# A fused top-k attention and feed-forward kernel: the feed-forward's steps from queues with conditions to a fixed list over four slots

## The chip, the cores and the metric

The kernel runs on one core of a Trainium2 chip. The metric is the device time of one execution in microseconds (us). Before the change the median of three runs is 1399.42 us (1398.67 to 1402.97).

The engines are named as in the profile: PE is TensorE (PEld its weight loads), DVE is VectorE, ACT is ScalarE, POOL is GpSimd, SP is SyncE, which here only issues DMAs. PE writes its results to PSUM, where the kernel's tiles take one bank (512 float32 columns) or two.

## What is computed

```python
# q, k, v: batch 8, heads 8, sequence 576, head size 64
scores = scale * np.matmul(q, k.transpose(0, 1, 3, 2))
kth = np.partition(scores, -32, axis=-1)[..., -32:-31]
scores = np.where(scores >= kth, scores, -1e9)
attn = np.exp(scores - np.max(scores, axis=-1, keepdims=True))
attn = attn / (np.sum(attn, axis=-1, keepdims=True) + 1e-09)
attn_out = np.matmul(attn, v)
# x: (4608 tokens, 512), the heads of a token side by side
h = x @ w_in            # w_in: 512 x 2048
g = h * np.cos(h)
out = g @ w_out         # w_out: 2048 x 512
```

The two weights come as float64; the kernel loads their words and rebuilds float32 from them ("decoding").

## The kernel before

**Units and slots.** The 4608 tokens are cut into 36 blocks of 128, the heads into 4 pairs. A unit is one block with one pair of heads: 128 rows, two times 576 scores. The 144 units run through a software pipeline with one unit a slot (`slot`, line 755); four slots make one block. The order in the program is the order in which each engine works, since the scheduling is manual. Slots are told apart by their number modulo 4 (0 to 3).

**Attention in a slot.** For the unit of slot i (`u`), DVE searches the 32 largest scores of each row: the row is folded in half into larger and lesser members (`fold_high`, line 261, makes the larger ones in `rest` from PSUM and from a copy `s`; POOL makes the lesser ones in `low` with `fold_sum`, line 279, and `fold_low`, line 287), then `topk_round` takes eight at a time with MAX8 and strikes them out with MATCH_REPLACE8: four searches in `rest`, and last two in `low`. The first slots that also decode weights (`BUSY`, slots 8 to 10) make `low` on DVE instead (`fold_now`, line 271). For the unit before (`w`), DVE merges the lists (`merge_first`, `merge_second`, lines 344 and 351), and ACT masks (`mask`, line 374) and exponentiates (`exponentials`, line 383), which leaves the sums of the rows; DVE ends the slot with the sums (line 395) and the reciprocal `rden` (line 400). For the unit before that (`x`), `send` (line 740) has POOL split the words of the probabilities and of the reciprocal into halves (`split`, line 405, two copies, lines 410 and 412), and SP writes them to memory and reads them back transposed into one of five places of `ring`. In the first six slots the transposes are done on PE instead (`turn`). PE makes the scores of two units in every second slot (slots 0 and 2, `scores`, line 235), and ACT copies those of the next unit out of PSUM (`take_scores`, line 250). In slot 2 PE multiplies the four transposed units of a block with V (P@V, `values`, line 456), and DVE scales the result into `xT` (`take_values`, line 481).

**PSUM.** Scores have two tiles of two banks, the tile `rim` (the last score columns and P@V) has two banks; two more banks, tag `mm`, serve both products of the feed-forward.

**Feed-forward.** The first product of a block (`ff1`, line 537) makes four banks of 128x512, each in two items; the second product (`ff2`, line 619) adds 16 chunks into one bank, in items of two chunks. ACT empties a bank of the first product with two instructions (`take_first`, line 566: `g`, and `x` as an integer, the number of turns). The argument of the cosine is reduced on POOL (`reduce_first`, line 590, makes `x` float, `reduce_second`, line 599, subtracts), ACT takes the sine (`sines`, line 602), POOL multiplies (`gate`, line 612), all on tiles of 128x1024, two for a block. `take_second` (line 638) scales the result and writes it out.

**What sets the order.** Items wait in the queues `first` and `second`; in each slot `feed` takes them by a plan, and `can_first` and `can_second` let an item go only if its inputs were made enough ticks ago:

```python
    plan = (
        ((0, 0), (1,), (1,)),
        ((0, 0), (1, 1), (0,)),
        ((0,), (1,), ()),
        ((1, 0, 0), (1, 1), ()),
    )
```

Here 0 is an item of the first product and 1 one of the second; the three groups of a slot stand ahead of the scores, behind the top-k's last round, and at the slot's end. Full banks are emptied wherever `take_banks` is called. After the last slot, `drain` and `forward` run what is left, with the cosine's argument and the gate on DVE.

**Weights.** `load_weights` (line 103) loads chunks, `decode_first` (ACT, at a slot's end), `decode_second` (DVE, line 151) and `decode_third` (POOL, line 160) rebuild them in this and the next slot.

Of the kernel before, what the change touches and what calls it, by code (L numbers as in the profile page):

```python
# [30 lines left out]
def kernel(  # L31
# [64 lines left out]
    ff = {"live": 0, "tick": 0, "now": 0, "end": False, "kind": 0, "half": 0, "open": 0, "late": False}  # L96
# [213 lines left out]
    def topk_first(u, w):  # L310

        u["top"] = tops[u["n"] % len(tops)]
        if w:
            merge_first(w)
        if u["n"] not in BUSY:
            fold_sum(u)
        fold_high(u)
        if w:
            merge_second(w)
        if u["n"] in BUSY:  # L320
            fold_now(u)
        topk_round(u, 0, [lambda: distances(w), lambda: None] if w else ())
# [82 lines left out]
    def split(u):  # L405


        s = u.pop("s").rearrange("p j k -> p (j k)").bitcast(U16)
        halves = work.tile([P, 2, 2 * S + P], U16, tag="halves", name="halves", bufs=1)
        nc.gpsimd.tensor_copy(out=halves[:, :, 0 : 2 * S], in_=s.rearrange("p (k h) -> p h k", h=2))  # L410
        rden = u.pop("rden").bitcast(U16).rearrange("p (j h) -> p h j", h=2)
        nc.gpsimd.tensor_copy(
            out=halves[:, :, 2 * S :].rearrange("p h (j d) -> p h j d", j=2),
            in_=rden.unsqueeze(3).to_broadcast([P, 2, 2, D]),
        )
        u["halves"] = halves
# [64 lines left out]
    def take_values(us):  # L481
# [23 lines left out]
        blk["left"] -= n  # L505
        blk["tick"] = ff["tick"]


    widths = [P] * (B * S // P)
    blocks, block_of = [], {}  # L510
    t0 = 0
    for w in widths:
        blk = {"t0": t0, "w": w, "left": 0, "g": [], "gated": []}
        for u in units:
            if t0 <= u["tok"] < t0 + w:
                block_of[u["tok"]] = blk
                blk["left"] += 1
        blocks.append(blk)
        t0 += w


    first = deque((blk, i) for blk in blocks for i in range(2 * NF * blk["w"] // 512))
    second = deque(
        (blk, i, f) for blk in blocks for i in range(blk["w"] // P) for f in range(0, NF, 2)
    )
    fresh = deque()
    waiting = deque()
    sined = deque()
    full = deque()

    def open_bank():

        if ff["open"] + len(full) == 2:
            take_banks()
        ff["open"] += 1

    def ff1(blk, i):
        w = blk["w"]
        nf = 256 // w
        part = i % 4  # L540
        if part == 0:
            blk["g"].append(ffw.tile([P, 1024], F32, tag="g", name="g", bufs=CHUNKS))
            blk["x"] = ffw.tile([P, 1024], F32, tag="x", name="x", bufs=XB)
            ff["live"] += 1
        if part % 2 == 0:
            open_bank()
            blk["mm"] = ps.tile([P, 512], F32, tag="mm", name="mm", bufs=2)
        g, mm = blk["g"][-1], blk["mm"]
        for a in range(nf):
            f = i * nf + a  # L550
            at = (part % 2 * nf + a) * w
            for c in range(NC):
                for r0 in range(0, P, D):
                    nc.tensor.matmul(  # L554
                        mm[r0 : r0 + D, at : at + w],
# [5 lines left out]
        if part % 2 == 0:  # L561
            return
        ff["open"] -= 1
        full.append((take_first, blk, g, blk["x"], mm, part // 2))

    def take_first(blk, g, x, mm, half):
        at = slice(half * 512, half * 512 + 512)
        nc.scalar.mul(out=g[:, at], in_=mm, mul=INV_2PI / UP)  # L568

        nc.scalar.activation(  # L570
            out=x[:, at].bitcast(I32), in_=mm, func=AF.Identity, bias=quarter, scale=INV_2PI / UP
        )
        if half == 1:
            fresh.append([blk, g, x, False, ff["now"] if ff["late"] else 0])

    def take_banks():
        while full:
            take, *what = full.popleft()
            take(*what)

    def reduce_first():

        if not fresh or (ff["late"] and not ff["end"] and fresh[0][4] == ff["now"]):
            return
        g, x = fresh[0][1:3]
        fresh[0][3] = True
# [5 lines left out]
        )  # L592

    def reduce_second():
        if not fresh or not fresh[0][3]:
            return
        blk, g, x, *_ = fresh.popleft()
        if not ff["end"]:
            nc.gpsimd.tensor_tensor(out=x, in0=g, in1=x, op=ALU.subtract)  # L599
        waiting.append((blk, g, x, ff["now"]))  # L600

    def sines(least):

        n = sum(c[3] < ff["now"] for c in waiting)
        if n == 0 or (n < least and waiting[0][3] + 2 > ff["now"]):
            return
        for _ in range(n):
            blk, g, x, _ = waiting.popleft()
            nc.scalar.activation(out=x, in_=x, func=AF.Sin, bias=halfpi, scale=TWO_PI_BELOW)
            sined.append((blk, g, x))  # L610

    def gate(n):
        for _ in range(min(n, len(sined))):
            blk, g, x = sined.popleft()
            eng = nc.vector if ff["end"] else nc.gpsimd
            eng.tensor_tensor(out=g, in0=g, in1=x, op=ALU.mult)  # L616
            blk["gated"].append(ff["tick"])

    def ff2(blk, i, f0):
        w = blk["w"]  # L620
        if f0 == 0:
            open_bank()
            blk["o"] = ps.tile([P, 512], F32, tag="mm", name="o2", bufs=2)
        o = blk["o"]
        per = 1024 // w
        for f in range(f0, f0 + 2):
            g = blk["g"][f // per]
            at = (f % per) * w + i * P
            for r0 in range(0, P, D):
                nc.tensor.matmul(  # L630
                    o[r0 : r0 + D], g[:, at + r0 : at + r0 + D], w_out[f], start=f == 0, stop=f == NF - 1
                )
        if f0 + 2 < NF:
            return
        ff["open"] -= 1
        full.append((take_second, blk, i, o))

    def take_second(blk, i, o):
        ob = ffw.tile([P, DM], F32, tag="ob", name="ob", bufs=1)
        nc.scalar.mul(out=ob, in_=o, mul=2.0 * math.pi / UP)  # L640
        row = blk["t0"] + i * P
        nc.scalar.dma_start(out=out[row : row + P, :], in_=ob)
        if i == blk["w"] // P - 1:
            ff["live"] -= len(blk["g"])
            blk["g"] = []

    def can_first():
        if not first:
            return False
        blk, i = first[0]  # L650
        if blk["left"] or ff["tick"] < blk["tick"] + 2 or wq["ready"] < (((i + 1) * (256 // blk["w"]) - 1) // FC + 1) * NC:
            return False
        return ff["now"] > NP + 2 and (i % 4 > 0 or ff["live"] + staged() < CHUNKS)

    def can_second():
        if not second or ff["now"] < 2 * NP + 3:
            return False
        blk, i, f = second[0]

        lag = 3 if ff["now"] < NU - NP else 2  # L660
        gated = sum(ff["tick"] >= t + lag for t in blk["gated"])
        return gated * 1024 // blk["w"] >= f + 2 and wq["ready"] >= NC * NF // FC + f + 2

    def item(kind):
        if not (can_first, can_second)[kind]():
            return False
        if kind == 0:
            ff1(*first.popleft())
        else:
            ff2(*second.popleft())  # L670
        return True

    def feed(*kinds):

        ff["tick"] += 1
        for kind in kinds:
            item(kind)

    def feed_any(n):

        ff["tick"] += 1
        for _ in range(n):
            kinds = (ff["kind"], 1 - ff["kind"])
            if second and second[0][2] == 0:
                kinds = (0, 1)
            if item(kinds[0]):
                kind = kinds[0]
            elif item(kinds[1]):
                kind = kinds[1]
            else:  # L690
                return
            if kind != ff["kind"] or ff["half"]:
                ff["kind"], ff["half"] = 1 - kind, 0
            else:
                ff["half"] = 1
# [44 lines left out]
    def send(x):  # L740

        split(x)
# [5 lines left out]
    plan = (  # L748
        ((0, 0), (1,), (1,)),
        ((0, 0), (1, 1), (0,)),  # L750
        ((0,), (1,), ()),
        ((1, 0, 0), (1, 1), ()),
    )

    def slot(i, u, w, x, z):
        n = (3, 4, 3, 4, 4, 3)[i] if i < NP + 2 else 2 if i != 2 * NP + 1 else 0
        if i < NP:
            for load, b, hp in at_once[i]:
                load(b, hp)
# [3 lines left out]
        ff["late"] = False  # L763
        topk_first(u, w)
# [18 lines left out]

        if i % 2:
            sines(1)
# [117 lines left out]
```

## Time and profile before

| | |
|---|---|
| median of three runs | 1399.42 us (1398.67 to 1402.97) |
| the profiled execution | 1399.15 us |
| its span, first to last instruction | 1397.0 us |
| granted TensorE clock, mean | 0.974 |
| ACT busy | 1140.6 us (82%) |
| POOL busy | 1169.3 us (84%) |
| matmuls / weight loads | 17024 / 17024 |

The span is what the profile of one execution covers; the 2.15 us to the device time lie outside of it. A line of the profile's groups names the source line, the engine, the operation, output and inputs by the program's names, their shapes and the count, then the busy time, the mean duration in ns, and the idle time ahead of them with what ended it. In a timeline a row has start, duration, engine, line and operation, and in brackets the idle time ahead and its releaser. Busy matmuls may overlap, since they are pipelined; an item's cost is read from the start of one to the start of the next.

### The profile page before, as it was taken

The numbers are of one execution on the slowest core, as the hardware profiler recorded it, in microseconds if no ns is written. First come the engines' busy times: TensorE is split into PE (matmuls) and PEld (weight loads), VectorE is DVE, ScalarE is ACT, GpSimd is POOL, SyncE is SP. The second block draws the span as 40 slices with busy tenths as digits, with TensorE's granted clock in tenths as the row PEclk, the third lists the DMA queues.
The fourth block names the chain that finished last, engine by engine and source line by source line (L and its number), as shares of the span: only waits on it lengthen the run. The fifth ranks groups of instructions, "written<-read, shape, count | busy, mean of one in ns | idle before, by whom it ended". The sixth has DMA issues, their size and how long they took to land.

```text
span 1397.0 us, 43804 instructions
## 1 busy us (share of the span) xinstructions
PE 1339.6 (96%) x17024; PEld 905.7 (65%) x17024; DVE 1334.2 (96%) x5004; ACT 1140.6 (82%) x2043; POOL 1169.3 (84%) x804
## 2 busy tenths in 40 slices
PE   5558999999999999999999999999999999999998
PEld 3445666666666666666666666666666666666664
DVE  7999999999999999999999999999999999999931
ACT  7987888888888888888888888888888888888842
POOL 4778988889988888888988889888888898998820
PEclk6688999999999999999999999999999999999999
DMA  9566776777575586658756567676766566555530
GB/s 303 180 203 179 196 191 167 202 175 206 160 179 160 154 198 177 175 161 200 185 157 170 159 178 191 177 164 171 211 163 172 160 171 163 160 146 157 157 103 16
DMA packets 427487, 240.86 MB, mean 172 GB/s; under 512 B 375952, under 2 KB 392592, under 8 KB 427280
## 3 DMA queue, kind: packets, MB, share of 16 engines
q1 hardware_dynamic: 420720, 224.22, 61.0%
q10 hardware_dynamic: 6560, 13.85, 2.9%
q8 instruction: 133, 2.18, 0.7%
q14 instruction: 74, 0.61, 0.1%
HBM read 45.09 MB, written 101.19 MB: 105 GB/s over the span
## 4 chain that ended last, share of the span: by engine, by line
PE 59%; DVE 35%; ACT 2%; DMA 2%; POOL 1%; issue 1%; SPq 0%; DVEq 0%; POOLq 0%; ACTq 0%
PE o L630 23%; PE mm L554 23%; DVE top L359 16%; DVE rest L364 10%; PE rim L475 7%; PE sc L242 5%; DVE low L364 3%; DVE rest L267 3%; PE rim L242 1%; DMA ring<-rows 1%; DMA rows<-halves 1%; DVE xT L491 0%; DVE top L347 0%; DVE w_out L151 0%; DVE top L352 0%
## 5 line engine op out<-in xcount | busy, mean ns | idle before, releaser
L554 PEld LDWEIGHTS mm<-xT,w_in 128*64 128x64 f32 x9216 | 512.8, 137 | 85.1 <-issue 57.2
L554 PE MATMUL mm<-xT,w_in 128*64 128x128 f32 x9216 | 528.7, 273 | 3.2 <-DVE xT L491 2.1
L630 PE MATMUL o<-w_out,g 128*64 128x512 f32 x2304 | 520.0, 594 | 0.0
L359 DVE MAX8 top<-rest 128x8 f32<-128x288 f32 x1152 | 479.5, 452 | 0.0
L364 DVE MATCH_REPLACE8 rest<-top,rest 128x288 f32<-128x288 f32 x864 | 377.0, 444 | 0.0
L378 ACT ACTIVATE s<-s,top 128x576 f32<-128x576 f32 x288 | 207.7, 768 | 160.8 <-DVE top L352 157.8
L630 PEld LDWEIGHTS o<-w_out,g 128*64 128x64 f32 x2304 | 158.6, 137 | 254.1 <-issue 253.1
L410 POOL COPY halves<-s 128x2304 uint16<-128x2304 uint16 x140 | 294.8, 2106 | 29.1 <-ACT s L387 26.0
L359 DVE MAX8 top<-low 128x8 f32<-128x288 f32 x576 | 242.6, 452 | 0.4 <-POOL low L292 0.4
L387 ACT ACTIVATE s<-s,nd 128x576 f32<-128x576 f32 x288 | 220.5, 769 | 1.1
L292 POOL TENSOR_TENSOR low<-low,rest 128x576 int32<-128x576 int32 x141 | 199.6, 1416 | 11.1
L283 POOL TENSOR_TENSOR low<-s 128x576 int32<-128x576 int32 x141 | 199.7, 1417 | 6.1 <-ACT s L259 6.1
L599 POOL TENSOR_TENSOR x<-g,x 128x1024 f32<-128x1024 f32 x68 | 161.6, 2376 | 5.7
L242 PE MATMUL sc<-k,q 64*64 64x448 f32 (+1 forms) x1120 | 146.9, 568 | 16.9 <-DVE low L275 10.2
L616 POOL TENSOR_TENSOR g<-g,x 128x1024 f32<-128x1024 f32 x68 | 161.7, 2378 | 0.0
L475 PE MATMUL rim<-ring,v 128*64 128x128 f32 (+1 forms) x2560 | 138.3, 267 | 0.0
L475 PEld LDWEIGHTS rim<-ring,v 128*64 128x64 f32 x2560 | 129.2, 139 | 6.5 <-issue 6.0
L253 ACT COPY s<-sc 128x896 f32<-128x896 f32 (+1 forms) x144 | 128.4, 891 | 3.1 <-PE sc L242 3.1
L257 ACT COPY s<-rim 64x256 f32<-64x256 f32 (+1 forms) x280 | 102.9, 368 | 29.5 <-PE rim L475 27.9
L364 DVE MATCH_REPLACE8 low<-top,low 128x288 f32<-128x288 f32 x288 | 125.8, 446 | 0.0
L267 DVE TENSOR_TENSOR rest<-sc,s 128x576 f32<-128x576 f32 x144 | 107.7, 748 | 7.0 <-ACT s L259 6.4
L568 ACT ACTIVATE g<-mm 128x512 f32<-128x512 f32 x144 | 85.2, 592 | 25.7 <-PE mm L554 23.2
(55 smaller groups left out, 1161.8 us busy)
## 6 DMA issues: line engine op xcount, KB each, us to landing
rows<-halves SPq DMA_DIRECT2D x140, 640.0 KB, 3.5
out_dram<-ob ACTq DMA_DIRECT2D x36, 256.0 KB, 2.2
q<-in_q_dram SPq DMA_DIRECT2D x31, 288.0 KB, 4.6
st<-in_moe_w_in_dram SPq DMA_DIRECT2D x16, 512.0 KB, 5.1
v<-in_v_dram SPq DMA_DIRECT2D x32, 256.0 KB, 4.2
k<-in_k_dram SPq DMA_DIRECT2D x31, 144.0 KB, 4.2
k<-in_k_dram SPq DMA_DIRECT2D x32, 128.0 KB, 4.7
st<-in_moe_w_out_dram SPq DMA_DIRECT2D x8, 512.0 KB, 4.7
```

The lines of the kernel that those rows point to most:

```text
L242: nc.tensor.matmul(to[r0 : r0 + rows, rim_bank(r0, j) if k0 else place(u["hp"], j), 0 : k1 - k0], st["q"][d, q0 : q0 + rows], st["k"][d, k ...
L283: nc.gpsimd.tensor_tensor(out=u["low"].bitcast(I32), in0=s[:, :, 0:HS], in1=s[:, :, HS:S], op=ALU.add)
L292: nc.gpsimd.tensor_tensor(out=low, in0=low, in1=u["rest"][:, :, HS:S].bitcast(I32), op=ALU.subtract)
L359: nc.vector.max(to[:, j], src[:, j])
L364: nc.vector.match_replace(rest[:, j], to[:, j], src[:, j], NEG)
L378: nc.scalar.activation(out=s[:, j], in_=s[:, j], func=AF.Prelu, bias=less[:, j], scale=1.0, alpha=FAR)
L387: nc.scalar.activation(out=s[:, j], in_=s[:, j], func=AF.Exp, bias=nd[:, j : j + 1], scale=SCALE, accum_out=den[:, j, 0:1],)
L410: nc.gpsimd.tensor_copy(out=halves[:, :, 0 : 2 * S], in_=s.rearrange("p (k h) -> p h k", h=2))
L475: nc.tensor.matmul(to[d, r], lhsT, rhs, start=(bank, j) not in begun, stop=c == NT - 1 and u in us[-2:] and r0 + rows == P,)
L554: nc.tensor.matmul(mm[r0 : r0 + D, at : at + w], w_in[f // FC][:, c, (f % FC) * P + r0 : (f % FC) * P + r0 + D], blk["xT"][:, c], start=c ...
L616: eng.tensor_tensor(out=g, in0=g, in1=x, op=ALU.mult)
L630: nc.tensor.matmul(o[r0 : r0 + D], g[:, at + r0 : at + r0 + D], w_out[f], start=f == 0, stop=f == NF - 1)
```

## The change

The queues, the plan and the conditions are gone. The feed-forward is a fixed list: a bank of the first product (`first_bank`, 32 matmuls) and a run of four chunks of the second (`second_run`) are called in named slots, and emptying, argument, sine and gate likewise. Argument and gate now work on 512 columns at a time, the sine still on 1024. For the block whose P@V is in slot 2, the list is: slot 2: bank 0; slot 3: bank 1, behind run 2 of the block before; slot 0: bank 2; slot 1: run 3 of the block before, bank 3, then run 0 of this block; next slot 2: scores, P@V, run 1; next slot 3: run 2. No feed-forward matmul stands ahead of the scores of a slot.

The emptying of bank 0 stands ahead of the score copies in slot 3, that of bank 1 right behind the mask in slot 0, those of banks 2 and 3 at the ends of slots 0 and 1. On POOL, argument 0 follows the split in slot 0, argument 1 the folds; in slot 1 gate 0 precedes the folds, gate 1 and argument 2 follow them; in slot 2 argument 3 precedes the folds, gates 2 and 3 follow. In slot 2 the sine precedes the score copies. `split` becomes two functions, which are called one behind the other. From slot 6 on, weight chunks are loaded in slots 6, 7, 9 and 11, two each (before: 6, 7, 8 and 10). `drain` is one fixed list for what is left.

```diff
-    def topk_first(u, w):
+    def topk_first(u, w, ahead=()):
         u["top"] = tops[u["n"] % len(tops)]
         if w:
             merge_first(w)
+        for step in ahead:
+            step()
...
+    def first_bank(b, k):
...
+        mm = blk["mm"][k] = ps.tile([P, 512], F32, tag="mm", name="mm", bufs=2)
+        for a in range(PER):
+            f = k * PER + a
+            assert wq["done"] >= (f // FC + 1) * NC
...
+    def argument(b, k):
...
+        g, x = half_of(blk["g"], k), half_of(blk["x"], k)
+        if ff["end"]:
+            nc.vector.tensor_tensor(out=x, in0=g, in1=x.bitcast(I32), op=ALU.subtract)
+            return
+        nc.gpsimd.tensor_scalar(
+            out=x, in0=x.bitcast(I32), scalar1=1.0, scalar2=0.0, op0=ALU.mult, op1=ALU.add
+        )
+        nc.gpsimd.tensor_tensor(out=x, in0=g, in1=x, op=ALU.subtract)
...
+    def gate(b, k):
...
+        g, x = half_of(blk["g"], k), half_of(blk["x"], k)
+        eng = nc.vector if ff["end"] else nc.gpsimd
+        eng.tensor_tensor(out=g, in0=g, in1=x, op=ALU.mult)
+
+    def second_run(b, r):
...
+        if r == 0:
+            blk["o"] = ps.tile([P, 512], F32, tag="mm", name="o2", bufs=2)
+        for f in range(r * PER, (r + 1) * PER):
...
     def slot(i, u, w, x, z):
-        n = (3, 4, 3, 4, 4, 3)[i] if i < NP + 2 else 2 if i != 2 * NP + 1 else 0
+        m, b = i % NP, (i - NP - 2) // NP
+        n = (3, 4, 3, 4, 4, 3, 2, 2, 0, 2, 0, 2)[i] if i < 3 * NP else 0
...
-        topk_first(u, w)
+        if m == 1:
+            gate(b, 0)
+        elif m == 0:
+            argument(b, 0)
+        topk_first(u, w, [lambda: argument(b - 1, 3)] if m == 2 else ())
         fold_low(u)
         topk_round(u, 1)
         topk_round(u, 2)
         if i > 1:
             decode_second(NP)
             decode_third()
-        reduce_first()
-        reduce_second()
-        made = scored.get(i, [])
-        if z:
-            take_banks()
-        feed(*((0, 0) if i == NP + 2 else plan[i % NP][0]))
-        for m in made:
-            scores(m)
+        for o in scored.get(i, []):
+            scores(o)
         if z:
             values(z)
-        if i % 2:
-            sines(1)
+        if m == 1:
+            gate(b, 1)
+            argument(b, 2)
+            second_run(b - 1, 3)
+        elif m == 2:
+            second_run(b - 1, 1)
+        elif m == 3:
+            second_run(b - 1, 2)
         if w:
             mask(w)
-        if i % NP != 3:
-            take_banks()
+        if m == 0:
+            take_first(b, 1)
+            argument(b, 1)
+            first_bank(b, 2)
+        elif m == 1:
+            take_second(b - 1)
+            first_bank(b, 3)
+            second_run(b, 0)
         if w:
             exponentials(w)
-        take_banks()
+        if m == 3:
+            take_first(b, 0)
+        elif m == 2:
+            sine(b - 1, 1)
+            gate(b - 1, 2)
+            gate(b - 1, 3)
         if i + 1 < NU:
             take_scores(units[i + 1])
...
         topk_round(u, 3, both(w), ahead)
...
-        ff["late"] = True
-        gate(1)
-        feed(*plan[i % NP][1])
-        take_banks()
+        if m == 2:
+            first_bank(b, 0)
+        elif m == 3:
+            first_bank(b, 1)
+        elif m == 0:
+            sine(b, 0)
+            take_first(b, 2)
+        elif m == 1:
+            take_first(b, 3)
         decode_first(NP)
-        reduce_first()
-        reduce_second()
-        feed(*plan[i % NP][2])
...
+    def drain():
+        b = NB - 2
+        ff["end"] = True
...
+        mask(w)
+        take_first(b, 1)
+        argument(b, 0)
+        argument(b, 1)
+        first_bank(b, 2)
+        exponentials(w)
+        sums(w)
+        reciprocal(w)
+        sine(b, 0)
+        gate(b, 0)
+        gate(b, 1)
+        take_first(b, 2)
+        second_run(b - 1, 3)
+        first_bank(b, 3)
+        take_second(b - 1)
+        send(w)
+        second_run(b, 0)
...
+        second_run(b, 1)
...
+        values(units[NU - 4 : NU - 2])
+        take_values(units[NU - 4 : NU - 2])
+        second_run(b, 2)
+        values(last_two)
+        take_values(last_two)
+        second_run(b, 3)
+        b += 1
...
+        for k in range(1, BANKS):
+            first_bank(b, k)
+            take_first(b, k)
+            argument(b, k)
...
+        for r in range(BANKS):
+            second_run(b, r)
+        take_second(b)
```

More of the change, by code (lines that the diff above doesn't have):

```diff
@@ L95 @@
     BUSY = range(8, 11)
-    ff = {"live": 0, "tick": 0, "now": 0, "end": False, "kind": 0, "half": 0, "open": 0, "late": False}
+    ff = {"live": 0, "end": False}
     wq = {"next": 0, "loaded": deque(), "second": deque(), "third": deque(), "done": 0, "ready": 0}
@@ L592, in reduce_first, with sine @@
         )
-    def reduce_second():
-        if not fresh or not fresh[0][3]:
+        nc.gpsimd.tensor_tensor(out=x, in0=g, in1=x, op=ALU.subtract)
+    def sine(b, t):
+        blk = block(b)
+        if blk is None:
             return
[L597 to L605, printed above, removed]
-            return
[L607 to L622, printed above, removed]
-            blk["o"] = ps.tile([P, 512], F32, tag="mm", name="o2", bufs=2)
[L624 to L628, printed above, removed]
+        x = blk["x"][t]
@@ L655, in can_second @@
[L655 to L695, printed above, removed]
+        ff["live"] -= len(blk.pop("g"))
```

195 lines of the change are left out of this document (73 added, 122 removed).

## The prediction

> **What bounds the kernel now.** I read the page first (busy time by engine), then windows by stage, the chain of waits, and the timelines of one steady group and of the end. A slot is one unit (two heads of 128 queries); four slots, 0 to 3, make a group, which ends in one block of 128 tokens for the feed-forward. P@V falls in slot 2.
>
> ```profile
> span 1397.0 us, 43804 instructions
> PE 1339.6 (96%) x17024; PEld 905.7 (65%) x17024; DVE 1334.2 (96%) x5004; ACT 1140.6 (82%) x2043; POOL 1169.3 (84%) x804
> L599 POOL TENSOR_TENSOR x<-g,x 128x1024 f32<-128x1024 f32 x68 | 161.6, 2376 | 5.7
> ```
>
> The windows (columns: busy time of PE, PEld, DVE, ACT, POOL; granted clock; DMA share; GB/s):
>
> ```profile
> 35.00:105.00 70.00, 39.69 (x446) 30.37 (x446) 70.00 (x251) 61.91 (x121) 54.09 (x42) 0.72 0.59 191
> 105.00:175.00 70.00, 63.08 (x772) 41.94 (x774) 67.56 (x251) 55.42 (x103) 61.12 (x42) 0.93 0.72 188
> 175.00:1331.90 1156.90, 1156.19 (x15086) 783.36 (x15084) 1156.90 (x4392) 978.57 (x1745) 1033.01 (x700) 1.00 0.66 173
> 1331.90:1397.00 65.10, 61.33 (x652) 37.49 (x648) 12.34 (x15) 18.94 (x29) 3.84 (x3) 1.00 0.19 54
> ```
>
> From 175 to 1331.9 us VectorE is busy 1156.90 of 1156.90: the top-k sets the pace and cannot go faster by any order. Only three amounts are open: 2.44 us of DVE idle between 105 and 175, the 65.1 us after the last top-k, in which TensorE works off its backlog (61.33 busy), and whatever waits a new order would add. TensorE has next to no room either. The chain (start, duration, engine, tile, count) over one group:
>
> ```profile
> 1133.71 4.08 PE rim L475 x80
> ...
> 1144.72 3.43 PE o L630 x16
> 1148.16 3.49 PE mm L554 x64
> 1153.75 3.58 PE o L630 x16
> ...
> 1164.26 3.49 PE mm L554 x64
> ...
> 1170.02 4.08 PE rim L475 x80
> ```
>
> A bank of the first product takes 3.49, a four-chunk run of the second 3.43, P@V 4.08. Two units' scores fill 1151.65 to 1153.75 (2.10) and 1167.75 to 1170.02 (2.27). Sum: 4 x 3.49 + 4 x 3.43 + 4.08 + 2.10 + 2.27 = 36.13, in a group of 1170.02 - 1133.71 = 36.31. TensorE has about 0.2 us per group to lose.
>
> **Steady state: is anything late for VectorE?** One slot 2 and the slot before it:
>
> ```profile
> 1231.67 0.23 DVE L347 TENSOR_REDUCE top<-top 128x34 f32<-128x68 f32 x1
> ...
> 1240.60 0.23 DVE L347 TENSOR_REDUCE top<-top 128x34 f32<-128x68 f32 x1
> 1240.69 0.40 POOL L412 COPY halves<-rden 128x256 uint16<-128x256 uint16 x1 [0.16 <-DVE rden L400]
> ...
> 1241.68 1.44 ACT L378 ACTIVATE s<-s,top 128x576 f32<-128x576 f32 x2 [1.25 <-DVE top L352]
> ...
> 1243.12 0.57 ACT L568 ACTIVATE g<-mm 128x512 f32<-128x512 f32 x1
> ...
> 1244.16 0.77 ACT L387 ACTIVATE s<-s,nd 128x576 f32<-128x576 f32 x1
> ...
> 1247.04 0.81 DVE L359 MAX8 top<-low 128x8 f32<-128x288 f32 x2
> 1247.15 0.74 ACT L257 COPY s<-rim 64x256 f32<-64x256 f32 x2 [0.58 <-PE rim L475]
> ...
> 1248.61 0.75 DVE L491 TENSOR_TENSOR xT<-rim,ring 128x256 f32<-128x256 f32 x2
> ...
> 1249.21 1.15 ACT L609 ACTIVATE x<-x,halfpi 128x1024 f32<-128x1024 f32 x1
> ...
> 1250.19 0.23 DVE L347 TENSOR_REDUCE top<-top 128x34 f32<-128x68 f32 x1
> ```
>
> A slot is 8.93 long, slot 2 is 9.59. Within a slot VectorE wants `low` from POOL at +6.44 (1247.04), and in slot 2 P@V's result at +8.01 (1248.61).
>
> *TensorE.* In the new list slot 1 ends with run 0 of the new block, so slot 2 has only scores and P@V ahead of xT. The second scores wait for VectorE's fold, about 0.9 into the slot (the releaser of 1241.68 is the reduce behind it); P@V then runs from about +1.9 to +6.0, 2.0 ahead of +8.01. Behind it come run 1, bank 0, run 2, bank 1: 6.0 + 2 x 3.43 + 2 x 3.49 = 19.84 after slot 2's start, which is 19.84 - 9.59 - 8.93 = 1.32 into slot 0. Since the second product's bank stays open from slot 1 to the next slot 1, one bank is left for the first product, and bank 2 must wait until ScalarE has emptied bank 1. That emptying stands right behind the mask: 1.08 + 1.44 + 1.04 (1241.68, 1243.12, 1244.16) = 3.56, while the scores cover TensorE until 1.32 + 2.10 = 3.42. The new wait is 0.14 a group, and closes once TensorE runs 0.14 later; queued behind it are run 3, bank 3, run 0 and the next scores. Cost: nothing, covered by the 0.2 of room and the 2.0 before xT. Without the scores as cover each emptying behind a mask would cost over 1 us.
>
> *ScalarE.* It issues the same instructions in another order. In slot 0 it does mask, emptying, exponentials, score copies and sine, as in the rows: 1241.68 to 1249.21 + 1.15, less the 0.58 waited, is 8.10; from +1.08 the sine ends at +9.18. In slot 2 the sine now stands ahead of the score copies; these wait there for P@V anyway (0.58 at 1247.15), so nothing is lost while P@V ends at +6.0.
>
> *POOL.* Here the change costs. Argument, subtraction and gate go from 1024 to 512 columns: 68 of each become 136, 204 instructions more. And most of them stand ahead of work that VectorE waits for. Durations, start to start:
>
> ```profile
> 1153.92 1.04 POOL L590 TENSOR_SCALAR x<-x 128x1024 f32<-128x1024 int32 x1 [0.54 <-ACT x L570]
> 1155.05 2.38 POOL L599 TENSOR_TENSOR x<-g,x 128x1024 f32<-128x1024 f32 x1
> 1157.37 2.11 POOL L410 COPY halves<-s 128x2304 uint16<-128x2304 uint16 x1
> 1159.41 0.41 POOL L412 COPY halves<-rden 128x256 uint16<-128x256 uint16 x1
> 1159.77 1.42 POOL L283 TENSOR_TENSOR low<-s 128x576 int32<-128x576 int32 x1
> 1161.27 1.42 POOL L292 TENSOR_TENSOR low<-low,rest 128x576 int32<-128x576 int32 x1
> 1162.64 2.37 POOL L616 TENSOR_TENSOR g<-g,x 128x1024 f32<-128x1024 f32 x1
> ```
>
> The split takes 2.04, the sums 0.36, both folds 2.87. With f the fixed part of an instruction, half a TENSOR_SCALAR is 0.52 + f/2 and 0.09 of gap, half a subtraction or gate 2.32/2 + f/2 = 1.16 + f/2; an argument is 1.77 + f. From the sums of slot 0 (0.09 after its start, 1240.69) to the last fold of slot 2, in the new order: 0.09 + 0.36, argument 0, 2.87, argument 1, 2.04, 0.36, gate 0, 2.87, gate 1, argument 2, 2.04, 0.36, argument 3, 1.50 + 1.42. That is 13.91 + 4 x (1.77 + f) + 2 x (1.16 + f/2) = 23.31 + 5f. Wanted: 2 x 8.93 + 6.44 = 24.30. The margin is 0.99 - 5f. (Gate 0 comes up at 9.26 + 2f, behind the sine's 9.18.) Rows for f: the two copies differ by 1.70 for 2048 elements, which leaves 0.41 - 256 x 0.00083 = 0.20; the smallest instruction,
>
> ```profile
> L880 POOL MEMSET const-bfloat16-1.0<- 128x1 bf16 x1 | 0.1, 101 | 0.0
> ```
>
> gives 0.10; and two 512-wide integer additions, one source strided, take 2.54, so 1.27 each, f/2 = 0.11, f = 0.22:
>
> ```profile
> 126.26 0.69 DVE L151 TENSOR_SCALAR w_out<-w_out 128x1024 int32<-128x1024 int32 x1
> ```
>
> ```profile
> 127.08 2.54 POOL L160 TENSOR_TENSOR w_out<-w_out,st 128x512 int32<-128x512 int32 x2 [1.97 <-issue]
> ```
>
> So the margin is +0.49 to -0.11. I take f = 0.20, nearest in kind: margin -0.01, a stall now and then, 0.03 a group. Over the 33 groups behind the start: +1.0 (bounds 0 and 3.6). Slot 3 has no feed-forward work on POOL, so no debt is carried on.
>
> The Trainium skill (GPSIMD Engine Reference, 3.1 Elementwise — side-by-side cycle accounting) gives 4497 ns for a two-input fp32 addition of 2048 elements and names a dispatch paid per instruction; it speaks against cutting instructions in half. With this trace's 2.376 for 1024 that is an estimate of f = 2 x 2.376 - 4.497 = 0.255, and the margin would be -0.29 instead of -0.01.
>
> **Start.** The last two weight chunks are now loaded in slot 11 and decoded in slot 12, a slot 0, ahead of argument 1, where the margin above is all there is: 2.54 on POOL, less the 0.69 by which their shift (126.26) lengthens VectorE's own slot: +1.85, once. Before, they fell into a slot 3. Against it stand the 2.44 of early DVE idle, which the new order may take away (0 to 2.44; nothing shows which); I take 1.0. Start: +0.85. The loads are as many as before, on the same queues; SP's order is unchanged.
>
> **End.**
>
> ```profile
> 1331.73 0.15 DVE L400 RECIPROCAL rden<-den 128x2 f32<-128x2 f32 x1
> ...
> 1333.31 0.45 PE L475 MATMUL rim<-ring,v_tail 64*64 64x128 f32 x8
> ...
> 1335.49 3.60 PE L630 MATMUL o<-w_out,g 128*64 128x512 f32 x16
> ...
> 1379.33 13.90 PE L630 MATMUL o<-w_out,g 128*64 128x512 f32 x64
> ...
> 1393.28 0.60 ACT L640 ACTIVATE ob<-o 128x512 f32<-128x512 f32 x1 [10.12 <-PE o L630]
> ```
>
> Before, TensorE ends 1393.23 - 1331.88 = 61.35 after the last top-k. After: 1.32 of bank 1; then a wait for its emptying, with no scores as cover (mask from about +0.5, 0.5 + 1.44 + 1.04 = 3.0, so 1.7); then 6 banks (20.94), 9 runs (30.87; before, 10 were left) and two half P@V (1335.49 - 1333.31 = 2.18 each): 1.32 + 1.7 + 56.17 = 59.2. I find no other wait: the halves gated last have two runs, 6.9 us, ahead of them. End: -2.1 (bounds -3.8 without the 1.7, and 0).
>
> **Sum.** 1397.0 - 2.1 + 0.85 + 1.0 = 1396.75; the profiled execution took 1399.15, 2.15 more than its span, and the median is 0.27 above it: 1399.2.
>
> **Rivals.**
> 1. *POOL is late in every group* (slower). It decides from f = 0.20 on. For it: the integer addition's 0.22, and no row of this width and type. Against: 0.10 and 0.20 from others. At f = 0.25, a little above the integer addition, the stall is 0.26 x 33 = 8.6 instead of 1.0: 1406.8. The skill's rule, above, would make it 0.29 x 33 = 9.6 by that estimate, 1407.8.
> 2. *The run ahead pushes P@V* (slower). The group's 36.31 less the sum's 36.13 leaves 0.18 that no matmul explains, changes between kinds. If the new order doubles them and the 0.14 stays open, TensorE needs 36.13 + 0.36 + 0.14 = 36.63 against VectorE's 3 x 8.93 + 9.59 = 36.38, and becomes the bound once the 2.0 before xT is used up: 0.25 x 33 - 2.0 = 6.2 more, 1405.4. Against: there are as many changes as before.
> 3. *The waits at both ends vanish* (faster): early idle 2.44 saved, the weights' 1.85 absorbed, the 1.7 covered, no stall: 1399.4 - 3.8 - 2.4 = 1393.2. For it: all these are single waits of uncertain place.
> 4. *No run is gained at the end*, since TensorE lags by as much: 1399.2 + 2.1 = 1401.3.
>
> **How the numbers follow.** A measurement of this kernel tells about 0.3% (4.2 us) from no change. Forecast 0.37 and rival 4 0.10 lie within it: 0.47. Rival 1 0.25 and rival 2 0.08: slower 0.33. Rival 3: faster 0.20. The range goes from rival 3 to just beyond rival 1, 1393 to 1408. The forecast's own range, with its terms' bounds, is 1395 to 1403.
>
> **What would show it.** Right: `low` never waited for in steady groups, or by a few tenths; half-width subtractions near 1.26 start to start; P@V ending some 6 us into slot 2; TensorE ending 59 us after the last top-k; waits in slots 13 and 14. Wrong: MAX8 on `low` waiting for POOL in every group (rival 1), or xT for P@V (rival 2); a backlog at the end of 57 or 61 us.

## The result, and the profile after

The changed kernel takes 1405.47 us (median of 7 runs, 1405.00 to 1405.71); the kernel before, run beside it, 1398.67 (7 runs). The ratio is 1.0047, 95% interval 1.0035 to 1.0058: slower by 6.8 us, and 6.3 above the forecast of 1399.2. The profiled execution took 1405.58.

The page of the changed kernel: span, busy times, the shares of the chain that ended last, and the half-width multiplications on POOL (busy, mean ns of one | idle ahead):

```profile
span 1403.4 us, 43913 instructions
PE 1340.8 (96%) x17024; PEld 900.8 (64%) x17024; DVE 1336.5 (95%) x5012; ACT 1136.6 (81%) x2043; POOL 1197.2 (85%) x1008
DVE 71%; ACT 20%; PE 4%; POOL 2%; issue 1%; ACTq 0%; POOLq 0%; DVEq 0%
L592 POOL TENSOR_TENSOR g<-g,x 128x512 f32<-128x512 f32 x136 | 172.6, 1280 | 16.2 <-ACT x L583 16.2
```

POOL is 28 us busier, with 204 more instructions. But POOL holds 2% of the chain, and ScalarE, which the forecast gave no cost, holds 20%.

The same windows as before, the borders between the last two moved to the new end of the last top-k (PE, PEld, DVE, ACT, POOL; clock; DMA share; GB/s):

```profile
35.00:105.00 70.00, 41.11 (x453) 30.96 (x453) 69.64 (x250) 59.51 (x119) 56.72 (x46) 0.72 0.60 192
105.00:175.00 70.00, 65.53 (x804) 41.83 (x802) 65.84 (x247) 58.06 (x106) 59.58 (x51) 0.98 0.72 192
175.00:1339.90 1164.90, 1159.52 (x15078) 780.11 (x15075) 1161.62 (x4398) 977.43 (x1750) 1061.02 (x892) 1.00 0.68 172
1339.90:1403.40 63.50, 58.22 (x638) 36.28 (x634) 12.25 (x24) 18.71 (x29) 2.85 (x3) 0.99 0.20 56
```

In the steady part VectorE now idles 1164.90 - 1161.62 = 3.28 us where it had idled nothing. To place the whole difference, the start of every slot was read off VectorE's timeline (the first TENSOR_REDUCE of a slot), in both traces:

| | before | after | difference | forecast |
|---|---|---|---|---|
| start of slot 15 | 159.11 | 160.95 | +1.84 | +0.85 |
| slot 15 to the end of the last top-k | 1172.7 | 1178.9 | +6.2 | +1.0 |
| from there to the end of the span | 65.1 | 63.5 | -1.6 | -2.1 |
| mean slot 3, 0 and 1 (32 of each) | 8.93 | 8.93 | 0.00 | 0 |
| mean slot 2 (32) | 9.590 | 9.784 | +0.194 | +0.03 |

All that the steady part lost is in slot 2: 32 x 0.194 = 6.2. And it is in every one of them: in the 32 groups slot 2 took 9.52 to 9.66 before and 9.71 to 9.86 after, without an outlier. One slot 2 of the changed kernel (start, duration, engine, line, operation):

```profile
1138.42 0.23 DVE L349 TENSOR_REDUCE top<-top 128x34 f32<-128x68 f32 x1
...
1141.01 3.71 PE L480 MATMUL rim<-ring,v 128*64 128x128 f32 x64
...
1142.71 1.28 ACT L583 ACT_TABLE_LOAD   x1
...
1143.34 1.42 POOL L292 TENSOR_TENSOR low<-low,rest 128x576 int32<-128x576 int32 x1
...
1144.01 1.15 ACT L583 ACTIVATE x<-x,halfpi 128x1024 f32<-128x1024 f32 x1
...
1144.86 0.81 DVE L361 MAX8 top<-low 128x8 f32<-128x288 f32 x2
...
1145.06 0.88 ACT L253 COPY s<-sc 128x896 f32<-128x896 f32 x1
...
1145.85 0.74 ACT L257 COPY s<-rim 64x256 f32<-64x256 f32 x2
...
1146.07 0.45 DVE L366 MATCH_REPLACE8 low<-top,low 128x288 f32<-128x288 f32 x1
...
1146.62 0.69 DVE L496 TENSOR_TENSOR xT<-rim,ring 128x512 f32<-128x512 f32 x1
...
1148.14 0.23 DVE L349 TENSOR_REDUCE top<-top 128x34 f32<-128x68 f32 x1
```

P@V ends at 1141.01 + 3.71 = 1144.72, 6.30 into the slot: as forecast, and 1.9 before xT. POOL's last fold ends at 1144.76, and `low` is searched at 1144.86 (+6.44) without a wait: as forecast. But xT starts at +8.20 instead of +8.02. What ends last before it is ScalarE: its two copies out of the tile `rim` (the last score columns of the next unit; below, "rim copies") end at 1145.85 + 0.74 = 1146.59. xT reads the same tile, and it waits for ScalarE behind these copies. It did so before the change too, where VectorE's list of waits has `DVE xT L491 <- ACT s L257: 0.7, 1, 0.7` and `DVE xT L499 <- ACT s L257: 1.2, 1, 1.2`, both in the start.

Why this hardly shows in a list of waits: xT starts 0.55 after the MATCH_REPLACE ahead of it. Where nothing is late it is 0.36 (1140.95 to 1141.31 in the first experiment, below), less than the instruction's own 0.43, since the next one on VectorE starts before it ends. Of the 0.19 lost, 0.10 is idle time (32 x 0.10 = 3.2, the 3.28 of the window), and neither the timeline nor the list names what it waited for; the rest is this overlap, lost, and it counts as busy. VectorE's list of waits (total, times, longest) has only these rows for `low` and the rim copies, and all of them fall ahead of slot 15:

```profile
DVE top L361 <- POOL low L292: 3.2, 3, 1.5
DVE xT L504 <- ACT s L257: 1.3, 1, 1.3
...
DVE xT L496 <- ACT s L257: 0.4, 1, 0.4
```

### The profile page after: what moved, and what is told of

Read it like the earlier page. It is cut to its first block, busy times and chain, and to the rows that moved or that the text cites. A ratio compares the mean times of both kernels' runs of the same rounds, so it can differ in the third digit from the quotient of the medians.

```text
span 1403.4 us, 43913 instructions
## 1 busy us (share of the span) xinstructions
PE 1340.8 (96%) x17024; PEld 900.8 (64%) x17024; DVE 1336.5 (95%) x5012; ACT 1136.6 (81%) x2043; POOL 1197.2 (85%) x1008
## 4 chain that ended last, share of the span: by engine, by line
DVE 71%; ACT 20%; PE 4%; POOL 2%; issue 1%; ACTq 0%; POOLq 0%; DVEq 0%
DVE top L361 33%; DVE rest L366 19%; DVE rest L267 7%; DVE low L366 6%; ACT s L389 4%; ACT s L380 4%; ACT L583 3%; ACT x L583 3%; PE o L606 2%; ACT s L253 2%; ACT s L257 2%; PE mm L543 2%; DVE xT L496 1%; DVE top L349 1%; DVE top L354 1%
## 5 line engine op out<-in xcount | busy, mean ns | idle before, releaser
L592 POOL TENSOR_TENSOR g<-g,x 128x512 f32<-128x512 f32 x136 | 172.6, 1280 | 16.2 <-ACT x L583 16.2
L575 POOL TENSOR_TENSOR x<-g,x 128x512 f32<-128x512 f32 x136 | 174.0, 1280 | 11.4
L257 ACT COPY s<-rim 64x256 f32<-64x256 f32 (+1 forms) x280 | 102.8, 367 | 3.4 <-PE rim L480 1.9
```

## The experiments

Times are medians; the ratio is to the kernel before, run on the same chip in the same rounds.

### 1. The rim copies first

```diff
-    def take_scores(u):
+    def take_scores(u, rim_first=False):
...
-        nc.scalar.copy(out=s[:, :, at:SB], in_=u["sc"][:, :, at:SB])
+        if not rim_first:
+            nc.scalar.copy(out=s[:, :, at:SB], in_=u["sc"][:, :, at:SB])
         ends = sc_ends[u["n"] % 2]
         for _, _, rows, r0 in u["parts"]:
...
+        if rim_first:
+            nc.scalar.copy(out=s[:, :, 0:SB], in_=u["sc"][:, :, 0:SB])
...
-            take_scores(units[i + 1])
+            take_scores(units[i + 1], m == 2)
```

> The changed kernel with one edit: in slot 2 the rim part of the score copies (64x256, two) stands ahead of the large copy (128x896). Theory 1: the 0.19 us that each slot 2 is longer than before is xT on VectorE, which waits for ScalarE's two rim copies; these end 8.17 us into the slot because the table load and the sine now stand ahead of all score copies. With the rim copies first they end 0.8 earlier: slot 2 is 9.5 to 9.65 again, span 1403.4 - 32 x 0.19 = about 1397.3, time about 1399.4. Rival: the 0.19 comes from POOL's half-width instructions (low late) or from VectorE itself: no change, 1405.4.

Measured: 1398.85 (10 runs), ratio 0.9998 (0.9988 to 1.0007). The mean slot 2 is 9.617; slot 15 to the last top-k takes 1173.7 (1178.9 in the changed kernel). One slot 2:

```profile
1133.29 0.23 DVE L352 TENSOR_REDUCE top<-top 128x34 f32<-128x68 f32 x1
...
1135.84 3.71 PE L483 MATMUL rim<-ring,v 128*64 128x128 f32 x64
...
1138.87 1.15 ACT L586 ACTIVATE x<-x,halfpi 128x1024 f32<-128x1024 f32 x1
...
1139.93 0.73 ACT L258 COPY s<-rim 64x256 f32<-64x256 f32 x2
...
1140.68 0.91 ACT L260 COPY s<-sc 128x896 f32<-128x896 f32 x1
...
1140.95 0.43 DVE L369 MATCH_REPLACE8 low<-top,low 128x288 f32<-128x288 f32 x1
...
1141.31 0.68 DVE L499 TENSOR_TENSOR xT<-rim,ring 128x512 f32<-128x512 f32 x1
```

P@V ends where it did (1139.55, +6.26) and the sine still stands ahead; the rim copies now end at +7.37, and xT starts at +8.02. Swapping two ScalarE copies gives back all of it. The 0.027 that are left in slot 2 are no steady loss: 30 of the 32 have the values of before, one took 10.20 and one 9.84. In both, `low` was late (searched at +7.11 and +6.68). The longer one goes back to a wait of POOL 26 us earlier, 2.74 for the DMA that writes `halves` out; POOL shows no idle time from there to the late search.

The edit also reaches the start: slot 10, a slot 2, takes 11.45 instead of 12.29.

### 2. The weights loaded as before

```diff
-        n = (3, 4, 3, 4, 4, 3, 2, 2, 0, 2, 0, 2)[i] if i < 3 * NP else 0
+        n = (3, 4, 3, 4, 4, 3, 2, 2, 2, 0, 2, 0)[i] if i < 3 * NP else 0
```

> The changed kernel with the weight chunks loaded in slots 6, 7, 8 and 10 again instead of 6, 7, 9 and 11. Theory: the 1.84 us that the changed kernel is behind at slot 15 are POOL's two late weight additions in slot 12, ahead of argument 1, so that low is late in slots 13 and 14. Then slots 13 and 14 lose their 1.6 and 0.6, and the time is 1.2 to 2.0 lower, about 1403.8. Rival: the early loss comes from the new places of the feed-forward's work in slots 10 to 14 whatever the weights do: no change, 1405.4.

Measured: 1405.16 (4 runs), ratio 1.0042 (1.0027 to 1.0057). Slot 13 falls from 10.53 to 8.93 and slot 14 from 11.07 to 10.59, so the additions did cause that stall. Slot 9 grows from 9.55 to 11.09 and slot 11 from 8.93 to 9.52, and slot 10 falls from 12.29 to 11.03. Slots 9 to 14 together take 60.47 instead of 61.90, and slot 15 starts at 160.04 instead of 160.95. The time shows 0.3 of this, less than the 1.2 to 2.0 expected. The profiled execution shows none (span 1404.0): behind its last matmul the span goes on for 4.9, against 3.7 in the changed kernel.

### 3. At the end, run 3 ahead of bank 2

```diff
         take_first(b, 1)
...
+        second_run(b - 1, 3)
         first_bank(b, 2)
...
+        take_second(b - 1)
...
-        take_first(b, 2)
-        second_run(b - 1, 3)
         first_bank(b, 3)
-        take_second(b - 1)
+        take_first(b, 2)
```

> The changed kernel with run 3 of block 33 ahead of bank 2 of block 34 in the drain (and the emptyings in the same order). Theory: TensorE's wait of 1.59 us for bank 1 to be emptied, right behind the last top-k, is covered by that run: the time is 1.6 lower, 1403.9. Rival: TensorE waits as long for something else a few microseconds later (the gate of block 34), so that nothing is gained: 1405.4.

Measured: 1404.31 (5 runs), ratio 1.0036 (1.0023 to 1.0049), 1.2 below the changed kernel. TensorE behind the last top-k, in the changed kernel first:

```profile
1343.07 3.71 PE L543 MATMUL mm<-xT,w_in 128*64 128x128 f32 x64 [1.59 <-ACT x L559]
...
1385.80 13.90 PE L606 MATMUL o<-w_out,g 128*64 128x512 f32 x64
```

and with run 3 ahead of bank 2:

```profile
1341.69 3.60 PE L606 MATMUL o<-w_out,g 128*64 128x512 f32 x16
1345.13 7.16 PE L543 MATMUL mm<-xT,w_in 128*64 128x128 f32 x128
...
1384.38 13.90 PE L606 MATMUL o<-w_out,g 128*64 128x512 f32 x64
```

The wait of 1.59 for the emptying of bank 1 is gone, with no other in its place: TensorE ends 1398.28 - 1340.28 = 58.0 behind the last top-k, against 1399.70 - 1339.88 = 59.8.

### 4. A little more work for POOL

The version of experiment 1 with three tiny clears (128x32) on POOL in slot 2, behind argument 3 and ahead of the folds:

```diff
+        if ahead:
+            for _ in range(3):
+                nc.gpsimd.memset(pad, 0.0)
```

> The kernel of the first run with three small memsets more on POOL (128x32, about 0.1 to 0.13 us each, results unused) between argument 3 and the folds of each slot 2. If POOL's work from the sums of slot 0 to low of slot 2 has the margin of about 0.1 us that the trace of the changed kernel shows (the last fold ends 0.10 ahead of the search in low), then 0.3 to 0.4 more stalls VectorE by 0.2 to 0.3 in every group: 6 to 10 us above the first run. Rival: POOL has more room than that, since its waits give it back: no more than 1 us above the first run.

Measured: 1410.27 (4 runs), ratio 1.0078 (1.0061 to 1.0095); the mean slot 2 is 9.934, 0.317 longer than in experiment 1. The clears, the fold behind them, and the search that waits for the folds, in one slot 2 that started at 1142.72:

```profile
1146.10 0.49 POOL L324 MEMSET pad<- 128x32 f32 x3
1146.55 1.42 POOL L286 TENSOR_TENSOR low<-s 128x576 int32<-128x576 int32 x1
```

```profile
1149.49 0.82 DVE L369 MAX8 top<-low 128x8 f32<-128x288 f32 x2 [0.24 <-POOL low L295]
```

The clears delay the folds by 0.45, and 0.32 of it reaches VectorE: POOL's margin is about 0.13 a group. Of the 11.4 that were lost against experiment 1 (6 to 10 expected), slot 2 has 32 x 0.317 = 10.1 and the start 1.5. That is the thin cover that the forecast had worked out; the change had used it up but not overdrawn it.

### 5. The sine back behind the score copies

```diff
-        elif m == 2:
-            sine(b - 1, 1)
-            gate(b - 1, 2)
-            gate(b - 1, 3)
         if i + 1 < NU:
             take_scores(units[i + 1])
+        if m == 2:
+            sine(b - 1, 1)
+            gate(b - 1, 2)
+            gate(b - 1, 3)
```

> The changed kernel with one thing moved: in slot 2 the second sine and the two gates that need it stand behind the score copies, as the sine did in the kernel before. Theory 1 (xT waits for ScalarE's rim copies, which stood behind the 1.3 of table load and 1.15 of sine): the rim copies now end about +7.1 into slot 2, xT is no longer late (about +8.05 instead of +8.20) and slot 2 loses no more than a few hundredths of the 0.19. But the sine ends some 2.7 later, about +9.5 (1138.42 to 1147.9), so gates 2 and 3 end about +12.0, while POOL has to begin the next split and folds at about +1.2 of slot 3 (+10.8 of slot 2) to be in time for low at +6.44. If so, the wait moves to low in slot 3: slot 3 grows by about 1.2 a group (some 10.1 instead of 8.93), 1405.5 - 6.2 + 38 = about 1437. If POOL can absorb it (the rival within this theory), 1399. Rival (slot 2 is longer for another reason, TensorE or POOL): slot 2 stays at 9.78 and the time is 1405 or more.

Measured: 1449.82 (4 runs), ratio 1.0356 (1.0341 to 1.0371). One group: the rim copies, the sine, the gates 2 and 3, and the search for `low` in slot 3, which started at 958.98:

```profile
955.46 0.74 ACT L257 COPY s<-rim 64x256 f32<-64x256 f32 x2 [1.25 <-PE rim L480]
...
957.52 1.15 ACT L583 ACTIVATE x<-x,halfpi 128x1024 f32<-128x1024 f32 x1
...
958.75 2.53 POOL L592 TENSOR_TENSOR g<-g,x 128x512 f32<-128x512 f32 x2 [3.02 <-ACT x L583]
...
966.56 0.82 DVE L361 MAX8 top<-low 128x8 f32<-128x288 f32 x2 [1.04 <-POOL low L292]
```

The rim copies end at 956.20, 1.14 ahead of xT, which no longer waits for them. But POOL stands 3.02 idle before the gates, which are ahead of the next split and folds in its order, and `low` comes 1.04 late in slot 3. The mean slot 3 is 10.30 (1.37 more, 1.2 expected), and since POOL has no room to catch up, slot 2 stays at 9.78 with POOL in ScalarE's place (`low` searched at +6.61). 32 x (1.37 + 0.17) is 49 of the 51 that were lost against experiment 1. The expectation of 1437 had slot 2 recover. Slot 2 at 9.78 and a time above 1405 were also the rival's sign, so by its numbers this experiment does not decide; the rows do, since xT's wait for ScalarE is gone, and so does experiment 1.

### 6. The last pair of weights one slot earlier

On the version of experiment 1:

```diff
-        n = (3, 4, 3, 4, 4, 3, 2, 2, 0, 2, 0, 2)[i] if i < 3 * NP else 0
+        n = (3, 4, 3, 4, 4, 3, 2, 2, 0, 2, 2, 0)[i] if i < 3 * NP else 0
```

> The version with the rim copies first (1398.9), and only the very last pair of weight chunks loaded one slot earlier: decoded in slot 11, a slot 3, in which POOL has no feed-forward work, instead of slot 12. Theory: slot 13 falls from 10.5 to 8.93 and slot 14 from 11.07 to about 10.5, slot 11 grows by 0.6 for VectorE's shift and slot 12 shrinks by as much; slot 15 starts about 2 us earlier than with the rim copies first alone (159.9), at 158; time 1396.8 to 1397.5. Rival (as in the run with both of the last pairs earlier): the weights' work is only paid in another slot, slot 10 or 11 grows by 1.5 to 2, and the time stays at 1398.9.

Measured: 1402.86 (11 runs), ratio 1.0023 (1.0013 to 1.0033): 4 us slower instead of 2 faster. Slots 11 to 14 go about as expected (9.53, 9.29, 8.93, 10.58; slot 12 was to shrink by 0.6 and shrank by 0.24), but slot 10 takes 16.84 instead of 11.45. What waited there (total, times, longest):

```profile
DVE xT L507 <- ACT s L258: 5.8, 1, 5.8
ACT s L258 <- PE rim L483: 5.3, 1, 5.3
...
PE rim L483 <- DMA ring<-rows: 3.8, 1, 3.8
```

P@V waits for its transposed rows, the rim copies behind it for P@V, xT for the copies. The transfers of 105 to 126 us (KB each, median us from issue to landing), with the loads in slot 10:

```profile
rows<-halves SPq DMA_DIRECT2D x2, 640.0 KB, 5.5
st<-in_moe_w_out_dram ACTq DMA_DIRECT2D x2, 512.0 KB, 6.8
ring<-rows SPq DMA_TRANSPOSE x2, 6.7
```

and in experiment 1, with the loads in slot 11:

```profile
rows<-halves SPq DMA_DIRECT2D x2, 640.0 KB, 3.4
st<-in_moe_w_out_dram ACTq DMA_DIRECT2D x2, 512.0 KB, 4.4
...
ring<-rows SPq DMA_TRANSPOSE x2, 4.9
```

The two loads of 512 KB were issued at 108.54 and 109.20. The transposes that P@V waited for began to be issued ahead of them, at 107.21, and took 8.4 to land instead of 4.8; a write of 640 KB behind them, at 110.12, took 7.4 instead of 3.4. The theory had counted the load's decoding on POOL and VectorE, and not its transfer. That the loads are the cause is borne out by experiment 8, which has them too (P@V waits 8.76), and by experiment 9, which does not.

### 7. One gate instead of two in slot 2

On the version of experiment 1; `gate_whole` multiplies the tile of 128x1024 in one instruction:

```diff
-            gate(b - 1, 2)
-            gate(b - 1, 3)
+            gate_whole(b - 1, 1)
```

> The version with the rim copies first (1398.9, slot 2 9.617 long on average against 9.590 before), and in slot 2 gates 2 and 3 as one full-width multiplication: one instruction fewer on POOL, f = 0.2 more of margin. Theory: the 0.027 that are left in slot 2 are POOL's (the forecast's 0.03 a group); slot 2 falls to 9.59 and the last top-k ends 0.9 us earlier; time about 1398. Rival: the 0.027 are xT's or TensorE's, and nothing changes, or the later end of half 2 (1.1 us) costs TensorE.

Measured: 1399.92 (11 runs), the kernel before beside it 1399.89, ratio 1.0000 (0.9992 to 1.0009). The mean slot 2 is 9.597, with 31 of 32 at the values of before and one at 9.78; the span is 1396.8 against 1397.1. Two stalls became one smaller one, 0.6 us of slot 2; the time cannot tell this from nothing. Experiment 9 has the same gate, and there `low` is late in three slots 2 again, so an effect of this edit is not shown.

### 8. All four together

Experiment 1, the order of experiment 3 at the end, the load of experiment 6 and the gate of experiment 7.

> Rim copies first, run 3 ahead of bank 2 after the last top-k, the last pair of weights one slot earlier, and one gate instead of two in slot 2. If the four add up: 1398.9 - 1.2 (the TensorE wait at the end) - 1.8 (start) - 0.9 (slot 2) = 1395.0, 0.26% faster than the kernel before. If the start's and the gate's gains don't come: 1397.7.

Measured: 1401.28 (12 runs, 1399.55 to 1405.76), ratio 1.0013 (1.0004 to 1.0021). Slot 10 took 20.27 in the profiled execution, which was the longest of the twelve (1405.76), so a typical one probably loses less there. Still, the load of experiment 6 costs more than the other three bring, as experiment 9 shows.

### 9. The three without the load

> Rim copies first, one gate in slot 2, run 3 ahead of bank 2 after the last top-k; the weight list as in the changed kernel. The run with all four lost 4 us and more in slot 10 to P@V's wait for its rows of values, which the earlier weight load had delayed; without that load the theory gives 1398.9 (rim copies first) - 0.6 (slot 2, 9.597 instead of 9.617) - 1.2 to -1.8 (the end) = 1396.5 to 1397.1, ratio 0.998 to 0.9985 of the kernel before; slot 10 back at 11.5, slot 15 at about 160, TensorE ending 58.0 after the last top-k. Rival (the three overlap, or the loss in the run with all four was not the load's): 1399 or more.

Measured: 1397.37 (7 runs, 1396.80 to 1398.91), the kernel before beside it 1401.31 (11 runs), ratio 0.9974 (0.9962 to 0.9985). Slot 10 is back at 11.47, slot 15 starts at 159.48, the span is 1395.2, and TensorE's last run of matmuls is:

```profile
1377.55 13.90 PE L617 MATMUL o<-w_out,g 128*64 128x512 f32 x64
```

TensorE ends 1391.45, which is 57.9 behind the last top-k at 1333.60. The mean slot 2 is 9.633, not 9.597: in three of them `low` was late, and in one P@V waited 1.25 for its rows.

So the fixed list, with one swap in slot 2, one at the end and the single gate, is faster than both kernels, by 0.15 to 0.38% against the one before. The ratio came out better than the 0.998 to 0.9985 expected, but the kernel before was slower in these rounds than in the others (1401.31 against 1398.67 to 1399.89). The profiled spans, 1395.2 and 1397.0, are only 0.13% apart.

## Why the prediction was wrong

The forecast was 1399.2 (1393 to 1408 as the range, "slower" at 0.33); the time was 1405.47. Against the span's sum, 1396.75, the profiled span is 6.65 more: 5.2 of it in the steady part, 1.0 at the start, 0.5 at the end.

**The step that failed** is the one on ScalarE: "In slot 2 the sine now stands ahead of the score copies; these wait there for P@V anyway (0.58 at 1247.15), so nothing is lost while P@V ends at +6.0." P@V did end at +6.3. The cover was the wrong one: it asked what the copies wait for, and not who waits for the copies. The rows that the prediction shows would have given the answer. Before, the rim copies waited 0.58 and ended at 1247.15 + 0.74 = 1247.89, 0.72 ahead of xT at 1248.61: together 1.30 of room. The change puts a sine of 1.15 ahead of them, and with it the loading of its table, which in the trace before stands between the copies and the sine:

```profile
1247.91 1.28 ACT L609 ACT_TABLE_LOAD   x1
```

The step counted neither. The change also takes the emptying of a bank away from there (1.04): 1.15 + 1.28 - 1.04 = 1.39. By these rows the copies end 0.09 past the +8.01 at which xT had started. In the trace after they end at +8.17, which is 0.16 past it, and xT follows 0.03 later: that is the 0.19. Experiment 1 shows that the place of the rim copies alone decides it: with P@V, sine and POOL where they were, 6.6 us came back.

**POOL's margin was right.** It was put at 0.99 - 5f with f = 0.20, that is -0.01. The half-width instruction takes 1.280, so f = 2 x 1.280 - 2.376 = 0.18 and the margin 0.07; experiment 4 measures about 0.13. The "stall now and then, 0.03 a group" is what experiment 1 shows once xT is out of the way: two stalls in 32 groups, 0.027 in the mean. In the changed kernel itself `low` was searched at +6.44 to +6.46 in every steady group, so the term of 1.0 was nothing there. That 0.03 and 0.027 agree is luck: the one was a guess, and the longer of the two stalls came from POOL's wait for a DMA, which the forecast did not have. By the Trainium skill (GPSIMD Engine Reference, 3.1 Elementwise — side-by-side cycle accounting) the estimate had been f = 0.255; that does not hold for this width here. The first rival, POOL late in every group, named 1406.8, close to what was measured, by a mechanism that did not occur: VectorE waited for `low` three times in the whole run, all of them ahead of slot 15. The second rival's 1405.4 was nearer still, and did not occur either. A time that fits is no evidence for its story.

**TensorE's path was right.** P@V at +6.3 instead of +6.0, no wait of xT for P@V, no sign of the second rival: slots 3, 0 and 1 are as long as before.

**The end was right in kind.** One run fewer was left, the new wait for the emptying of bank 1 came (1.59, forecast 1.7) and went with experiment 3; TensorE ended 59.8 behind the last top-k, forecast 59.2. The gain was 1.6 instead of 2.1. The fourth rival is out.

**The start was half right.** The stall that the last weights cause is there: the search for `low` waits in slots 13 and 14,

```profile
147.39 0.82 DVE L361 MAX8 top<-low 128x8 f32<-128x288 f32 x2 [1.51 <-POOL low L292]
...
157.79 0.82 DVE L361 MAX8 top<-low 128x8 f32<-128x288 f32 x2 [1.37 <-POOL low L292]
```

and experiments 2 and 6 take it out of slot 13. Slots 13 and 14 grew by 1.61 + 0.61 = 2.2, where 1.85 was forecast. Against that, 1.0 was to come back from VectorE's early idle time. Slots 9 to 12 gave back 0.6 (40.30 instead of 40.90); the 0.2 lost ahead of slot 9 says little, since slot 1 starts anywhere between 16.17 and 17.22 in the traces. And part of the start's loss is the failed step again: in slot 10 xT waits 1.28 for the rim copies, and the slot takes 12.29 instead of 11.57. With the rim copies first it takes 11.45 (11.45 to 11.51 in experiments 1, 4, 7 and 9, 12.28 in experiment 3 without), so 0.84 of the 1.84 at the start are theirs. The third rival (waits vanish at both ends) had this as its ground, and the traces show the opposite: between 105 and 175 VectorE idles 4.16 instead of 2.44. What the start could be with another list was not settled: the list of before took 1.4 less in slots 9 to 14, but the time shows only 0.3, and that of experiment 6 was slower.

## What to carry to other kernels

When an instruction is moved ahead of others on an engine, sum that engine's whole sequence up to the moved-past instructions, table loads included, and compare it with the moment when their consumers want them; that they wait for something now is only part of the room. Two readers of one tile can be ordered by the program, so look for the consumer behind the tile's other reader too. A loss of 0.2 us that repeats in every group hardly shows in a list of waits, since half of it can be lost overlap: compare the mean length of each kind of slot instead.

## What the runs showed of the hardware that was not expected

A wait of TensorE was followed by slow matmuls, which cost another 2.7 us. In experiment 6 P@V waited 3.79 for its rows and then took 6.43 where it takes 3.71 (start, duration, and the wait in brackets):

```profile
115.68 0.69 PE L483 MATMUL rim<-ring,v_tail 64*64 64x128 f32 x4 [3.79 <-DMA ring<-rows]
116.30 6.43 PE L483 MATMUL rim<-ring,v 128*64 128x128 f32 x64
```

The granted clock was low just then (the number behind POOL's), 0.63 between 116 and 124:

```profile
116.00:124.00 8.00, 8.00 (x76) 6.83 (x74) 2.17 (x10) 2.70 (x5) 6.59 (x5) 0.63 0.43 95
```

while the version of experiment 1, without the load and the wait, has 1.00 in the same window:

```profile
116.00:124.00 8.00, 8.00 (x92) 5.14 (x90) 7.56 (x31) 6.15 (x10) 8.00 (x7) 1.00 0.72 208
```

In experiment 8, where P@V waited 8.76, it was 0.59 there.

Whether the length of the wait matters can be read at another place. At about 104 us, all versions of the changed kernel have a run of 16 matmuls that waits for the gate. Experiment 6 first, then experiment 1:

```profile
104.00 5.35 PE L609 MATMUL o<-w_out,g 128*64 128x512 f32 x16 [3.25 <-POOL g L595]
```

```profile
104.02 3.65 PE L609 MATMUL o<-w_out,g 128*64 128x512 f32 x16 [2.27 <-POOL g L595]
```

In the changed kernel and in experiments 3 to 7 and 9 this wait took 3.07 to 3.48. There the granted clock was 0.59 to 0.70 between 104 and 108, and the 16 matmuls took 5.35. In experiments 1, 2 and 8 it took 2.26 or 2.27, with a clock of 1.00 and 3.65 for the matmuls. So the longer wait goes with the lower clock. Its length is not all: around 142 us a wait of 2.10 in experiment 7 was followed by 0.57 and 5.38 for 64 matmuls, and waits of 2.01 to 2.15 in the changed kernel and experiments 1, 3, 4 and 9 by 1.00 and 3.71. That the wait brings the clock down stays an inference, since no edit set its length alone.
